# Attention scores and values issued for four units at a time, with ScalarE's work reordered around them, in a top-k attention and MLP kernel

## The chip, the cores and the metric

The kernel runs on one core of a Trainium2 chip. A core has a matmul engine (TensorE, PE in the profile, with its weight loads listed as PEld), a vector engine (VectorE, DVE), a scalar engine (ScalarE, ACT), a third elementwise engine (GpSimd, POOL) and a sync engine (SP) that issues transfers. They run side by side, each through its own instructions in order, and wait for each other on semaphores. The metric is the device time of one execution in microseconds (us): less is better.

## The reference

Two blocks follow one another. The attention has 8 batches, 8 heads, 576 tokens and 64 values per head, and keeps the 32 largest scores of every row. Its output, with the heads side by side, is the input of an MLP with 4608 tokens, 512 inputs, 2048 hidden values and a leaky ReLU. All is float32.

```python
def _attn_ref(q, k, v):                       # each (8, 8, 576, 64)
    scores = scale * np.matmul(q, k.transpose(0, 1, 3, 2))
    kth = np.partition(scores, -32, axis=-1)[..., -32:-31]
    scores = np.where(scores >= kth, scores, -1000000000.0)
    scores = scores - np.max(scores, axis=-1, keepdims=True)
    attn = np.exp(scores)
    attn = attn / (np.sum(attn, axis=-1, keepdims=True) + 1e-09)
    return np.matmul(attn, v).astype(np.float32)

def _moe_ref(x, w_in, w_out):                 # (4608, 512), (512, 2048), (2048, 512)
    h = x @ w_in
    g = np.maximum(0.01 * h, h)
    return (g @ w_out).astype(np.float32)
```

## The kernel before

The work is cut into 144 **units**. A unit is 128 rows of queries for two heads of one batch (a "pair" of heads), so two score blocks of 128 x 576. As 576 is four times 128 and 64 over, each batch also has two units of 64 rows for four heads. The MLP takes its tokens in 19 **chunks**, two of 128 and then 17 of 256; a chunk of 256 tokens needs the values of eight units.

One loop runs over steps. In step s, DVE picks the top 32 of unit s, POOL masks unit s-1, ACT takes its exponents, and unit s-2 is normalized, split in 16-bit halves, written out and read back transposed (wT). The values of a unit come some steps later. In between, the MLP is fed in small pieces: a budget says how much of it PE gets at each of the seven places ("slots") of a step. Each engine receives its instructions in the order in which the program names them.

Scores go to PSUM in two parts per unit, a "wide" (352 keys) and a "narrow" one (224 keys), and ACT copies them to SBUF. PSUM holds two "wide" buffers of two banks each, one "narrow" one of two banks, and two banks for the MLP. The values use one bank of a "wide" buffer too:

```python
    def scores(us):                                   # two units
        narrow = ps_sc.tile([P, 2, 512], F32, name="narrow")
        ps = {}
        for k, u in enumerate(us):
            wide = ps_sc.tile([P, 2, 512], F32, name="wide", bufs=2)
            ps[u] = ((wide[:, :, 0:WIDE], 0, WIDE),
                     (narrow[:, :, k * NARROW:(k + 1) * NARROW], WIDE, S))
        order = ((us[0], 0), (us[0], 1), (us[1], 1), (us[1], 0))
        for u, part in order:
            ...
                    nc.tensor.matmul(to[r0:r0 + u.rows, i, :], qt[d, u.q0:u.q0 + u.rows],     # L220
                                     kt[d, k0:k1], start=True, stop=True)
        for u in us:
            u.both = work.tile([P, 2, S], F32, name="s_sb", bufs=5)
            ...
        for u, part in order:
            nc.scalar.copy(u.both[:, :, k0:k1], to)                                          # L227

    def top_k(u):              # DVE; four parts, each ended by a yield
        ...                    # max and min of the halves of a row (L250), then four times
                               # MAX8 (L255), with MATCH_REPLACE8 (L258) between them
    def mask(u, i): ...        # POOL, L266 to L269
    def exponents(u, i): ...   # ACT, L272: exp(s_sb), and its sum z
    def sums(u): ...           # ACT, L277: ze = z + 1e-9
    def reciprocals(u): ...    # DVE, L281: rz = 1 / ze
    def normalize(u, i): ...   # ACT, L284: s_sb * rz

    def transpose(u):
        for h in range(2):
            split = work.tile([P, 2 * S], U16, name="split", bufs=2)
            nc.scalar.copy(split, pairs[:, :, h])                                            # L293
            nc.sync.dma_start(apart[:, h, :], split)
        u.wT = work.tile([P, 2 * NKC - 1, P], F32, name="wT", bufs=3)
        nc.sync.dma_start_transpose(out=u.wT.bitcast(U16), in_=...)                          # L296

    def weigh_values(u, po): ...   # PE, L333: 2 x 5 products of wT and v, two side by side
    def keep_values(u, po): ...    # ACT, L347: po to x, the MLP's input

    def mlp(ch):                   # a generator: one piece up to each yield
        for f0 in range(0, NFC, 2):
            ph = ps_ml.tile([P, 2, CHMAX], F32, name="ph", tag="ml")
            ...                    # PE, L389: 4 pieces of ph
            nc.scalar.activation(gT[...], ph[...], AF.Prelu, alpha=SLOPE)                    # L395
            yield 2 * max(n, 225)
        for r0 in range(0, n, P):
            pz = ps_ml.tile([P, 512], F32, name="pz", tag="ml")
            ...                    # PE, L401: 8 pieces of pz
            nc.scalar.copy(o_sb[0:m], pz[0:m, 0:DMODEL])                                     # L410
```

The schedule, from step 20 on (`HURRY` = 20; earlier steps differ in order, not in work):

```python
    def values_at(n):                        # step and place of unit n's values
        if n < UNHURRIED: return (n | 1) + LAG + 1, MIDDLE
        return (n | 1) + LAG - ((n | 1) in HURRIED), END             # LAG = 3

    def slot_budget(s):
        after = [at for (at, _), _ in ready_at if at >= s]           # when chunks become ready
        until = after[0] if after else s
        if len(after) >= len(CHUNKS) - EARLY: return EARLY_SHARE
        return backlog[0] / ((until + 1 - s) * SLOTS)                # SLOTS = 7

        for s in range(len(steps) + LAG + 1):
            cur, old, older, new = unit(s), unit(s - 1), unit(s - 2), ()
            if s % 2 == 0:
                new = [u for u in steps[s + 2:s + 4] if u]
            ...
            slot()                           # one part of top_k(cur)
            if old: mask(old, 0); mask(old, 1)
            if older: weights_of(older)      # reciprocals, normalize twice
            mlp_steps(budget)
            ...
            slot()
            mlp_steps(budget)
            if old: exponents(old, 0)
            if older: transpose(older)
            slot()
            mlp_steps(budget); mlp_steps(budget)
            slot()
            mlp_steps(budget)
            if old: exponents(old, 1); sums(old)
            keep(values(s, END), s, END)     # two units' values, and their copies to x
            if new: scores(new)              # two units' scores
            budget = slot_budget(s + 1)
            mlp_steps(budget); mlp_steps(budget)
            load_more(s)
```

Before the loop, the MLP's weights are rounded in 16 pieces (`round_weights`, on POOL, ACT, DVE and PE).

Of the kernel before, what the change touches and what calls it, by code (L numbers as in the profile page):

```python
# [20 lines left out]
def kernel(  # L21
# [37 lines left out]
    const = ctx.enter_context(tc.tile_pool(name="const", bufs=1))  # L59
    xpool = ctx.enter_context(tc.tile_pool(name="xpool", bufs=2))  # L60
    loads = ctx.enter_context(tc.tile_pool(name="loads", bufs=LOADED))
    raws = ctx.enter_context(tc.tile_pool(name="raws", bufs=3))
    work = ctx.enter_context(tc.tile_pool(name="work", bufs=2))
    small = ctx.enter_context(tc.tile_pool(name="small", bufs=5))
    halves = ctx.enter_context(tc.tile_pool(name="halves", bufs=3, space=bass.MemoryType.DRAM))
# [15 lines left out]
    w_out = [const.tile([P, 4, DMODEL], F32, name=f"w_out{c}") for c in range(NFC // 4)]  # L81
    gT = const.tile([P, NFC, CHMAX], F32, name="gT")

    NPIECE = 2 * HP * DFF // WCH
# [3 lines left out]
    def piece(n):  # L90
# [4 lines left out]
        f = 2 * (n - NPIECE // 2)  # L95
        return w_out[f // 4][:, f % 4:f % 4 + 2, :].rearrange("p g n -> p (g n)")

    raw_of = {}

    def load_weights(n):  # L100
        if n >= NPIECE:
            return
        if not AS_WORDS:
            nc.sync.dma_start(piece(n), weights[n])
            return
        raw_of[n] = raws.tile([P, WCH, 4], U16, name="raw")
        nc.sync.dma_start(raw_of[n].rearrange("p n w -> p (n w)"), weights[n])

    def round_weights(n):

        raw = raw_of.pop(n)
        dst = piece(n)
        mid = raw[:, :, 2]
        low = raw.rearrange("p n w -> p (n w)").bitcast(U32).rearrange("p (n w) -> p n w", w=2)[:, :, 0]
        top = raws.tile([P, WCH], U16, name="top", bufs=2)
        scale = raws.tile([P, WCH], U16, name="scale", bufs=2)  # L120
        parts = work.tile([P, 2 * NKC - 1, P], F32, name="wT", bufs=3)
        parts = parts.rearrange("p c n -> p (c n)").bitcast(U16)
        m_top, m_low = parts[:, 0:WCH], parts[:, WCH:2 * WCH].bitcast(BF16)
        nc.gpsimd.tensor_copy(top, raw[:, :, 3])
        nc.scalar.activation(dst, mid, AF.Copy, bias=-7.0 - 2.0 ** -16, scale=2.0 ** -20)

        nc.scalar.activation(m_low, low, AF.Copy, bias=128.0, scale=2.0 ** -29)
        yield
        nc.vector.tensor_scalar(scale, top, 4, 0x7FF, ALU.logical_shift_right, ALU.bitwise_and)  # L129
        if n < NPIECE - 2:  # L130

            nc.scalar.activation(scale.bitcast(BF16), scale, AF.Exp, bias=least, scale=LN2)
        else:

            nc.vector.tensor_scalar(scale, scale, 1151.0, 896.0, ALU.min, ALU.max)
            nc.vector.tensor_scalar(scale, scale, 896.0, 128.0, ALU.subtract, ALU.mult)
        nc.vector.tensor_scalar(m_top, top, 0xF, 0x3F80, ALU.bitwise_and, ALU.bitwise_or)
        nc.vector.tensor_scalar(top, top, 0x8000, None, ALU.bitwise_and)  # L138
        if n < NPIECE - 4 or n % 2 == 0:
            tag, bufs = ("wide", 2) if n < NPIECE - 4 else ("narrow", 1)  # L140
            pw = ps_sc.tile([P, 2, 512], F32, name=tag, bufs=bufs)
            sums = [(pw[:, h, :], h * 512) for h in range(2)]
            ends = [(pw.rearrange("p h n -> p (h n)"), 0)]
        else:
            ends = sums = [(ps_ml.tile([P, 512], F32, name="pw", tag="ml"), h * 512) for h in range(2)]
        for pw, c in sums:
            at = slice(c, c + 512)
            nc.tensor.matmul(pw, ident_top, m_top[:, at].bitcast(BF16), start=True, stop=False)
            nc.tensor.matmul(pw, ident, dst[:, at], start=False, stop=False)
            nc.tensor.matmul(pw, ident_low, m_low[:, at], start=False, stop=True)  # L150
        yield
        nc.vector.tensor_tensor(scale, scale, top, ALU.bitwise_or)  # L152
        for pw, c in ends:
            at = slice(c, c + pw.shape[-1])
            nc.vector.tensor_tensor(dst[:, at], pw, scale[:, at].bitcast(BF16), ALU.mult)  # L155
# [5 lines left out]
    def load_qk(pi):  # L161
        if pi % (LOADED + 3) < LOADED:
            qt = loads.tile([P, S], F32, name="qt")
            kt = loads.tile([P, S], F32, name="kt")
        else:
            raw = raws.tile([P, WCH, 4], U16, name="raw").rearrange("p n w -> p (n w)").bitcast(F32)
            qt, kt = raw[:, 0:S], raw[:, S:2 * S]
        nc.sync.dma_start(qt, qT[pi])
        nc.sync.dma_start(kt, kT[pi])
        qk_of[pi] = qt, kt  # L170
# [32 lines left out]
    def scores(us):  # L203
# [16 lines left out]
                    nc.tensor.matmul(to[r0:r0 + u.rows, i, :], qt[d, u.q0:u.q0 + u.rows],  # L220
                                     kt[d, k0:k1], start=True, stop=True)
        for u in us:
            u.both = work.tile([P, 2, S], F32, name="s_sb", bufs=5)
            u.s = [u.both[:, i, :] for i in range(2)]
        for u, part in order:
            to, k0, k1 = ps[u][part]
            nc.scalar.copy(u.both[:, :, k0:k1], to)  # L227
# [1 line left out]
    def first_scores(u):  # L229

        ps = [ps_sc.tile([P, 2, 512], F32, name="wide", bufs=2) for i in range(2)]
        for half in range(2):
            for i, pi, side, r0 in u.parts:
                qt, kt = qk_of[pi]
                d = slice(side * D, (side + 1) * D)
                nc.tensor.matmul(ps[i][:, half, 0:HS], qt[d, u.q0:u.q0 + P],
                                 kt[d, half * HS:(half + 1) * HS], start=True, stop=True)
        u.both = work.tile([P, 2, S], F32, name="s_sb", bufs=5)
        u.s = [u.both[:, i, :] for i in range(2)]
        for i in range(2):  # L240
            nc.scalar.copy(u.s[i].rearrange("p (h n) -> p h n", h=2), ps[i][:, :, 0:HS])

# [40 lines left out]
    def normalize(u, i):  # L283
        nc.scalar.activation(u.s[i], u.s[i], AF.Copy, bias=0.0, scale=u.rz[:, i:i + 1])  # L284

    def transpose(u):


        pairs = u.both.rearrange("p i n -> p (i n)").bitcast(U16).rearrange("p (n h) -> p n h", h=2)
# [1 line left out]
        for h in range(2):  # L291
            split = work.tile([P, 2 * S], U16, name="split", bufs=2)
            nc.scalar.copy(split, pairs[:, :, h])  # L293
            nc.sync.dma_start(apart[:, h, :], split)
        u.wT = work.tile([P, 2 * NKC - 1, P], F32, name="wT", bufs=3)
        nc.sync.dma_start_transpose(out=u.wT.bitcast(U16), in_=apart.rearrange("p h n -> (p h) n"))  # L296

    def transpose_in_haste(u):
# [8 lines left out]
            u.parts_T.append((c0, c1, pt))  # L307

    def keep_transposed(u):
        u.wT = work.tile([P, 2 * NKC - 1, P], F32, name="wT", bufs=3)  # L310
        for c0, c1, pt in u.parts_T:
            nc.scalar.copy(u.wT[:, c0:c1, :], pt[:, 0:c1 - c0, :])

# [37 lines left out]
    def hidden_of_few(ch, x):  # L351

        g_of = {}
        for j in range(NFC // 4):
            ph = ps_ml.tile([P, 512], F32, name="ph", tag="ml")
            for c in range(HP):
                nc.tensor.matmul(ph, x[c][:, 0:P], w_in[c][:, j * 512:(j + 1) * 512],
                                 start=(c == 0), stop=(c == HP - 1))
                if c == 1:
                    yield 2 * 512  # L360
            g_of[j] = raws.tile([P, 2 * DMODEL], U16, name="scale", bufs=2).bitcast(F32)
            nc.scalar.activation(g_of[j], ph, AF.Prelu, alpha=SLOPE)  # L362
            yield 2 * 512
            if j:
# [77 lines left out]
    HURRIED = (15, 23, 31)  # L442
    HASTY = (14, 15, 23, 31)
    UNHURRIED = 14
    MIDDLE, END = 0, 1

    def values_at(n):

        if n < UNHURRIED:
            return (n | 1) + LAG + 1, MIDDLE  # L450
        return (n | 1) + LAG - ((n | 1) in HURRIED), END
# [17 lines left out]
                ready.append(ch)  # L469
                backlog[0] += mlp_cost(ch)  # L470

    def slot_budget(s):

        after = [at for (at, _), _ in ready_at if at >= s]
        until = after[0] if after else s
        if len(after) >= len(CHUNKS) - EARLY:
            return EARLY_SHARE
        return backlog[0] / ((until + 1 - s) * SLOTS)

    EARLY_SHARE = 500  # L480
    SLOTS = 7

    with tc.manual_schedule():
        last = {p: n for n, u in enumerate(steps) for p in u.pairs}

        def load_more(s):

            for of, load, n, lag in ((v_of, load_v, LOADED_V, LAG + 1), (qk_of, load_qk, LOADED + 3, 8)):
                while len(of) < NPAIR and (len(of) < n or last[len(of) - n] + lag <= s):
                    load(len(of))  # L490
                    if lag > LAG + 1 and len(of) > n:
                        break


        for n in range(3):
            load_weights(n)
        rounding = {}
        for n in range(NPIECE + 2):
            for i in (n, n - 1, n - 2) if AS_WORDS else ():
                if 0 <= i < NPIECE:  # L500
                    if i == n:
                        rounding[i] = round_weights(i)
                    next(rounding[i], None)
            load_weights(n + 3)
# [15 lines left out]
        def values(*place):  # L520
            due = [u for n, u in enumerate(steps) if values_at(n) == place]
            if due:
                po = ps_sc.tile([P, 2, 512], F32, name="wide", bufs=2)[:, 0, 0:2 * P]
                po = po.rearrange("p (u n) -> p u n", u=2)
            else:
                return ()
            for n, u in enumerate(due):
# [7 lines left out]

        for s in range(len(steps) + LAG + 1):
            cur, old, older, new = unit(s), unit(s - 1), unit(s - 2), ()
            if s % 2 == 0:
                new = [u for u in steps[s + 2:s + 4] if u]
            picks = top_k(cur) if cur else iter(())  # L540
            budget = slot_budget(s)

# [7 lines left out]
            if old:  # L550
                mask(old, 0)
                mask(old, 1)
            late = s < HURRY and not {s - 1, s - 2} & set(HURRIED)
            if older and not late and not at_first:
                weights_of(older)
            mlp_steps(budget)
# [7 lines left out]
            if s - 2 in HASTY:  # L564
                transpose_in_haste(older)
            mlp_steps(budget)
            if old:
                exponents(old, 0)
            if older:
                keep_transposed(older) if s - 2 in HASTY else transpose(older)  # L570
            slot()
            mlp_steps(budget)
            mlp_steps(budget)
            slot()
            mlp_steps(budget)
            if old:
                exponents(old, 1)
                sums(old)
            if not at_once:
                keep(weighed, s, MIDDLE)  # L580
            if new and s < HURRY:
# [2 lines left out]
            if new and s >= HURRY:  # L584
                scores(new)
            budget = slot_budget(s + 1)
            mlp_steps(budget)
            mlp_steps(budget)
            load_more(s)
        mlp_steps(1e9)  # L590
# [58 lines left out]
```

## Time and profile before

| | |
|---|---|
| time, median of three runs | 1474.29 us (1473.32 to 1475.12) |
| span of the profiled run | 1471.0 us |
| mean granted clock of PE | 0.979 |
| bytes moved | 222.29 MB, mean 151 GB/s |
| median from issue to landing: split out, transposed back | 2.1 us, 4.6 us |

The profile lists one execution. A line such as L333 is a line of the kernel; a group is written as line, engine, operation, output<-input, shapes, count. PE lists every float32 matmul twice[...]. The table by stage gives, for each stretch of time, the busy time of PE, PEld, DVE, ACT and POOL with the number of instructions, then the granted clock, the share of the transfer engines and GB/s. The timeline gives start, length, engine, line and count, and in brackets how long the engine had been idle before and who released it. A line of the waits names who waited, for whom, how long in all, how often and the longest. The ends of matmuls are modelled, so PE is better read from start to start.

### The profile page before, as it was taken

The numbers are of one execution on the slowest core, as the hardware profiler recorded it, in microseconds if no ns is written. First come the engines' busy times: TensorE is split into PE (matmuls) and PEld (weight loads), VectorE is DVE, ScalarE is ACT, GpSimd is POOL, SyncE is SP. The second block draws the span as 40 slices with busy tenths as digits, with TensorE's granted clock in tenths as the row PEclk, the third lists the DMA queues.
The fourth block names the chain that finished last, engine by engine and source line by source line (L and its number), as shares of the span: only waits on it lengthen the run. The fifth ranks groups of instructions, "written<-read, shape, count | busy, mean of one in ns | idle before, by whom it ended". The sixth has DMA issues, their size and how long they took to land.

```text
span 1471.0 us, 24094 instructions
## 1 busy us (share of the span) xinstructions
PE 1395.6 (95%) x8066; PEld 928.7 (63%) x8068; DVE 1322.4 (90%) x3400; ACT 1095.7 (74%) x1979; POOL 1096.5 (75%) x743
## 2 busy tenths in 40 slices
PE   7717989999999999999999999999999999999999
PEld 2304547676766666666666666767676767676674
DVE  7999999999999999999999999999999999999600
ACT  8657877877787777777777777787877787877720
POOL 3188877888788888787878788878787888787700
PEclk9957999999999999999999999999999999999999
DMA  9725443654367554666557545565457555654510
GB/s 343 287 73 137 137 113 89 172 168 137 105 169 214 131 147 130 182 175 152 137 164 198 154 128 144 161 198 144 130 164 207 143 134 130 170 136 134 145 47 14
DMA packets 388795, 222.29 MB, mean 151 GB/s; under 512 B 333888, under 2 KB 333888, under 8 KB 386624
## 3 DMA queue, kind: packets, MB, share of 16 engines
q1 hardware_dynamic: 388672, 220.77, 53.1%
q8 instruction: 63, 1.03, 0.3%
q14 instruction: 60, 0.49, 0.1%
HBM read 46.14 MB, written 92.01 MB: 94 GB/s over the span
## 4 chain that ended last, share of the span: by engine, by line
PE 86%; DVE 11%; DMA 1%; ACT 1%; issue 1%; POOL 0%; DVEq 0%; SPq 0%; ACTq 0%
PE pz L401 33%; PE ph L389 32%; PE wide L333 11%; PE wide L220 6%; DVE tops L255 4%; PE narrow L220 3%; DVE pairs L258 3%; DMA raw<-in_weights_dram 1%; DVE pairs L250 1%; DVE w_in L155 1%; DVE scale L152 1%; DMA wT<-apart 0%; DVE w_out L155 0%; DVE scale L129 0%; DVE top L138 0%
## 5 line engine op out<-in xcount | busy, mean ns | idle before, releaser
L268 POOL TENSOR_SCALAR pen<-s_sb,tops 128x576 f32<-128x576 f32 x288 | 637.5, 2213 | 209.6 <-DVE tops L255 116.8
L255 DVE MAX8 tops<-pairs 128x8 f32<-128x288 f32 (+1 forms) x1152 | 636.5, 592 | 0.0
L401 PE MATMUL pz<-w_out,gT 128*128 128x512 f32 x1152 | 510.7, 597 | 4.9 <-ACT scale L362 4.9
L389 PE MATMUL ph<-x,w_in 128*128 128x256 f32 x2176 | 481.1, 381 | 0.0
L258 DVE MATCH_REPLACE8 pairs<-tops,pairs 128x288 f32<-128x288 f32 (+1 forms) x864 | 460.6, 539 | 0.0
L389 PEld LDWEIGHTS ph<-x,w_in 128*128 128x128 f32 x2176 | 410.7, 190 | 77.1 <-issue 22.9
L269 POOL TENSOR_TENSOR s_sb<-s_sb,pen 128x576 f32<-128x576 f32 x288 | 406.9, 1413 | 24.1
L401 PEld LDWEIGHTS pz<-w_out,gT 128*128 128x128 f32 x1152 | 215.6, 190 | 269.7 <-issue 263.5
L293 ACT COPY split<-s_sb 128x1152 uint16<-128x1152 uint16 x280 | 306.9, 1145 | 0.0
L284 ACT ACTIVATE s_sb<-s_sb,rz 128x576 f32<-128x576 f32 x288 | 207.0, 769 | 42.2 <-DVE rz L281 42.2
L272 ACT ACTIVATE s_sb<-s_sb,nbias 128x576 f32<-128x576 f32 x288 | 221.0, 767 | 12.5 <-POOL s_sb L269 12.5
L250 DVE TENSOR_TENSOR pairs<-s_sb 128x576 f32<-128x576 f32 x288 | 213.4, 780 | 9.9
L333 PEld LDWEIGHTS wide<-wT,vt 128*64 128x64 f32 x3200 | 161.7, 139 | 65.5 <-ACT s_sb L227 27.0
L333 PE MATMUL wide<-wT,vt 128*64 128x128 f32 (+1 forms) x3200 | 179.0, 268 | 22.8 <-ACT s_sb L227 21.2
L395 ACT ACTIVATE gT<-ph 128x512 f32<-128x512 f32 x136 | 80.6, 592 | 80.1 <-PE ph L389 80.1
L347 ACT COPY x<-wide 128x128 f32<-128x128 f32 (+1 forms) x160 | 32.1, 260 | 128.2 <-PE wide L333 128.2
L227 ACT COPY s_sb<-wide 128x704 f32<-128x704 f32 x142 | 107.2, 755 | 25.4 <-PE wide L220 25.3
L220 PE MATMUL wide<-kt,qt 64*128 64x352 f32 (+1 forms) x392 | 76.5, 504 | 26.5 <-ACT s_sb L227 23.6
L227 ACT COPY s_sb<-narrow 128x448 f32<-128x448 f32 x142 | 68.7, 537 | 1.3 <-PE narrow L220 0.6
L410 ACT COPY o_sb<-pz 128x512 f32<-128x512 f32 x36 | 21.1, 585 | 59.2 <-PE pz L401 59.2
L281 DVE RECIPROCAL rz<-ze 128x2 f32<-128x2 f32 x144 | 22.5, 156 | 46.1 <-ACT ze L277 45.9
L258 DVE MATCH_VALUE_LOAD pairs<-tops,pairs 128x8 f32 x864 | 63.4, 73 | 0.0
(63 smaller groups left out, 620.5 us busy)
## 6 DMA issues: line engine op xcount, KB each, us to landing
apart<-split SPq DMA_DIRECT2D x280, 288.0 KB, 2.1
raw<-in_weights_dram SPq DMA_DIRECT2D x16, 1024.0 KB, 7.2
vt<-in_vk_dram SPq DMA_DIRECT2D x32, 320.0 KB, 3.5
out_dram<-o_sb SPq DMA_DIRECT2D x36, 256.0 KB, 2.0
qt<-in_qT_dram SPq DMA_DIRECT2D x20, 288.0 KB, 3.1
kt<-in_kT_dram SPq DMA_DIRECT2D x20, 288.0 KB, 3.5
raw<-in_qT_dram SPq DMA_DIRECT2D x12, 288.0 KB, 3.1
raw<-in_kT_dram SPq DMA_DIRECT2D x12, 288.0 KB, 3.6
```

Source lines behind the costliest of these rows:

```text
L220: nc.tensor.matmul(to[r0:r0 + u.rows, i, :], qt[d, u.q0:u.q0 + u.rows], kt[d, k0:k1], start=True, stop=True)
L250: nc.vector.tensor_tensor(pairs[:, :, n, :], u.both[:, :, 0:HS], u.both[:, :, HS:S], op)
L255: nc.vector.max(out=u.tops[:, i, r, :], in_=rest[i])
L258: nc.vector.match_replace(out=rest[i], in_to_replace=u.tops[:, i, r, :], in_values=rest[i], imm_value=LOWEST)
L268: nc.gpsimd.tensor_scalar(pen, u.s[i], u.tops[:, i, ROUNDS - 1, 7:8], MASKED, ALU.is_lt, ALU.mult)
L269: nc.gpsimd.tensor_tensor(u.s[i], u.s[i], pen, ALU.add)
L272: nc.scalar.activation(u.s[i], u.s[i], AF.Exp, bias=u.nbias[:, i:i + 1], scale=SCALE, accum_out=u.z[:, i:i + 1])
L284: nc.scalar.activation(u.s[i], u.s[i], AF.Copy, bias=0.0, scale=u.rz[:, i:i + 1])
L293: nc.scalar.copy(split, pairs[:, :, h])
L333: nc.tensor.matmul(po[side * D:(side + 1) * D, o, :], vt[:, c, side, :], u.wT[:, c + side * NKC if c + 1 < NKC else c, r:r + n], start=(c ...
L389: nc.tensor.matmul(ph[:, i, 0:n], w_in[c][:, f * P:(f + 1) * P], x[c][:, 0:n], start=(c == 0), stop=(c == HP - 1),)
L401: nc.tensor.matmul(pz[0:m, 0:DMODEL], gT[:, f, r0:r0 + m], w_out[f // 4][:, f % 4, :], start=(f == 0), stop=(f == NFC - 1),)
```

## The change

Scores and values of the units from 40 on come in groups of four. In every fourth step, after the second slot, a block is issued: the scores of the next two units, the values of four finished units (those still go to one "wide" buffer, whose bank they now fill), then the scores of two more. Into this block, in ACT's order, are put the splits of unit s-2 and the exponents of unit s-1, so that ACT has work while PE makes the values, and the copies of the values right behind. The purpose is to change less often between the shapes of matmul, and to keep ACT from standing idle at the values. The budget counts in slots rather than steps, and the pieces of the MLP stand between ACT's single operations.

To have room for more units in flight, the buffers that the weights' rounding leaves free (`words`, `tops_scales`) serve later as two more wT buffers, a sixth score buffer and the extra buffers for q and k, which were rotating tiles before. Cut to its core:

```diff
+    words = raws.tile([P, 3, WCH * 4], U16, name="words")
+    tops_scales = raws.tile([P, 4, WCH], U16, name="tops_scales")
+    later = ...                                    # five buffers within words
+    wT_bufs = [three tiles] + [two of later]       # unit n uses wT_bufs[n % 5]
+    s_bufs = [five tiles] + [one in tops_scales]   # n % 6 from unit 30 on, n % 5 before
 ...
-        nc.gpsimd.tensor_copy(top, raw[:, :, 3])       # round_weights: ahead of ACT's two
+        nc.gpsimd.tensor_copy(top, raw[:, :, 3])       # behind them, in a part of its own
 ...
-    def transpose(u):
+    def transpose(u, between):
             nc.scalar.copy(split, pairs[:, :, h])
             nc.sync.dma_start(apart[:, h, :], split)
+            if h == 0:
+                between()
 ...
+    MIDDLE, END, AMID = 0, 1, 2
+    FOURS = 40
     def values_at(n):
+        if n >= FOURS - 4:
+            return ((n | 1) if len(steps[n].pairs) > 1 and n % 4 < 2 else (n | 3)) + LAG + 1, AMID
 ...
-    def slot_budget(s):
+    def slot_budget(s, done=0):
+        ends = [at * SLOTS + (SLOTS_AHEAD if place == AMID else SLOTS) for (at, place), _ in ready_at]
+        left = [end - s * SLOTS - done for end in ends if end > s * SLOTS + done]
 ...
+        return backlog[0] / (left[0] if left else SLOTS)
+    SLOTS_AHEAD = 2
 ...
-            if s % 2 == 0:
-                new = [u for u in steps[s + 2:s + 4] if u]
+            if s % 2 == 0 and s + 2 < FOURS:
+                new = steps[s + 2:s + 4]
+            four = s % 4 == 3 and s + 1 >= FOURS
 ...
-            late = s < HURRY and not {s - 1, s - 2} & set(HURRIED)
+            late = s < HURRY and not {s - 1, s - 2} & set(HURRIED) or s % 4 == 0 and s >= FOURS
             if older and not late and not at_first:
                 weights_of(older)                  # with late: behind the second slot
             mlp_steps(budget)
 ...
             mlp_steps(budget)
-            if old: exponents(old, 0)
-            if older: ... transpose(older)
+            if four:
+                if unit(s + 1):
+                    scores(steps[s + 1:s + 3])
+                weighed = values(s, AMID)
+                if older:
+                    transpose(older, lambda: None)
+                if old:
+                    exponents(old, 0)
+                keep(weighed, s, AMID)
+                if old:
+                    exponents(old, 1)
+                    sums(old)
+                if unit(s + 3):
+                    scores(steps[s + 3:s + 5])
+                budget = slot_budget(s, SLOTS_AHEAD)
+                mlp_steps(budget)
+                mlp_steps(budget)
+            else:
+                if old:
+                    exponents(old, 0)
+                mlp_steps(budget)
+                keep(values(s, AMID), s, AMID)
+                if older: ... transpose(older, lambda: mlp_steps(budget))
+            slot()
             slot()
             mlp_steps(budget)
-            mlp_steps(budget)
-            slot()
-            mlp_steps(budget)
-            if old:
+            if old and not four:
                 exponents(old, 1)
                 sums(old)
+            mlp_steps(budget)
```

## The prediction

> **What bounds the kernel now.** I read the page first, then the busy time by stage, then the timeline of the matmul engine over one turn, then the waits.
>
> ```profile
> PE 1395.6 (95%) x8066; PEld 928.7 (63%) x8068; DVE 1322.4 (90%) x3400; ACT 1095.7 (74%) x1979; POOL 1096.5 (75%) x743
> PE 86%; DVE 11%; DMA 1%; ACT 1%; issue 1%; POOL 0%; DVEq 0%; SPq 0%; ACTq 0%
> ```
>
> PE is busiest and 86% of the chain that ended last. The table by stage (PE, PEld, DVE, ACT, POOL busy) shows where:
>
> ```profile
> 80.00:120.00 40.00, 10.84 (x70) 8.19 (x72) 39.62 (x101) 26.75 (x49) 33.26 (x24) 0.54 0.38 104
> 754.20:901.70 147.50, 147.50 (x866) 100.54 (x865) 141.50 (x369) 116.28 (x212) 119.71 (x81) 1.00 0.58 159
> ```
>
> Until about 200 us DVE (top-k) is full and PE has little to do; after that PE never idles, and DVE is free for only 6.0 of 147.5 us (16 units), about 0.37 us per unit. The change acts almost wholly in this second stage. One turn there, and the last MLP piece in the chain:
>
> ```profile
> 827.84 11.39 PE L389 MATMUL ph<-x,w_in 128*128 128x256 f32 x52
> 839.16 2.40 PE L333 MATMUL wide<-wT,vt 128*64 128x128 f32 x40
> 841.49 0.86 PE L220 MATMUL wide<-kt,qt 64*128 64x352 f32 x4
> 842.19 0.92 PE L220 MATMUL narrow<-kt,qt 64*128 64x224 f32 x8
> 842.94 0.76 PE L220 MATMUL wide<-kt,qt 64*128 64x352 f32 x4
> 843.63 14.94 PE L389 MATMUL ph<-x,w_in 128*128 128x256 f32 x68
> ...
> 1412.41 27.63 PE ph L389 x128
> 1440.04 27.48 PE pz L401 x64
> ```
>
> Read from start to start. 256 columns take 27.63/128 = 0.216 us and 512 take 27.48/64 = 0.429 us, so a column takes 0.834 ns plus 2.4 ns per matmul. A pair of values (20 times two side by side, 128 columns) should then take 20 x 0.109 = 2.18 us; it takes 841.49 - 839.16 = 2.33. A pair of scores (four matmuls of 352 and four of 224 columns, each beside its twin) should take 1.94; it takes 2.14. The MLP run of 52 takes 11.32 for 11.23, that of 68 (to the next values at 858.50) 14.87 for 14.68: about 0.1 us at each end. So a turn loses 0.15 + 0.20 + 0.19 = 0.54 us in its three changes of shape, 0.18 each. Check: a chunk of 256 tokens (8 units) should take 27.63 + 27.48 + 4 x (2.18 + 1.94) + 4 x 0.54 = 73.8 us, and 16 units take 147.5.
>
> Now who waits for whom inside that stage (ACT's and DVE's timelines, then the waits from 606.65 to 1197.2):
>
> ```profile
> 833.21 0.77 ACT L272 ACTIVATE s_sb<-s_sb,nbias 128x576 f32<-128x576 f32 x1
> 833.87 0.19 ACT L272 ACTIVATION_READ_ACCUMULATOR s_sb<-s_sb,nbias 128x1 f32 x1
> 834.10 0.20 ACT L277 ACTIVATE ze<-z 128x2 f32<-128x2 f32 x1
> ...
> 834.33 0.17 DVE L281 RECIPROCAL rz<-ze 128x2 f32<-128x2 f32 x1 [1.06 <-ACT ze L277]
> ...
> ACT x L347 <- PE wide L333: 65.0, 32, 3.1
> DVE rz L281 <- ACT ze L277: 19.9, 30, 1.2
> ```
>
> DVE's spare time is spent waiting for ze, the sum that ACT makes at the end of a step: DVE is tied to ACT, and ACT (in program order) to PE.
>
> **What the Trainium skill says.** "TensorEngine Tiling (Array Packing)", section Key Properties: changing the tiling mode drains the engine. The trace agrees: 0.18 us per change, as above. "TensorE: Matmul & The Clock Gate", in its section on the array of 32x32 parts: ScalarE and VectorE queues are strict FIFO, matmuls stay in program order. The trace agrees: at 834.33 the reciprocal waits 1.06 us and the MAX8 behind it, which needs no ze, waits too. "PSUM — Partial Sum Buffer", Specifications: a bank holds 512 FP32 values per partition; so the values of four units (4 x 128 columns) fill the one bank used of a "wide" buffer. No run shows that yet.
>
> **The change, part by part.**
>
> *Fewer changes of shape.* For units 40 to 143 a block is scores of two, values of four, scores of two: four changes of shape for four units, where two turns have six. Units 36 to 143 (values) and 40 to 143 (scores) now take 52 turns x 3 and two of values alone x 2 = 160 changes. After: the block at step 39 has scores alone (2), the 25 at 43 to 139 have 4, the values of a half-group at 57, 93 and 129 stand alone (2 each), the last two blocks 3: 111. So 49 x 0.18 = **8.8 us** less work for PE. A block takes 2 x 2.14 + 40 x 0.109 + 0.15 = 8.8 us, and four units take 27.6 (half a chunk of MLP) + 8.8 + 0.2 = 36.5 us.
>
> *Uneven steps.* The MLP is dealt out in 7 slots a step, 55.1/56 = 0.98 us of PE each. Now every second step has 6.9 us of PE, the others 11.5. After, three steps of 6.9 us follow one of 15.7, while DVE still needs 8.9 us for each. Take T as the start of the block in step s (s = 43, 51, ...: the MLP half that makes ph follows), and follow the chain:
> - PE starts MLP at T + 8.9 and ends the third ph tile (3.46 us each) at T + 19.3.
> - Counting pieces by the new budget, that tile's Prelu is emitted in slot 5 of step s+1, just ahead of the second exponent and ze. ACT: wait 0.2, Prelu 0.49, exponent with sum 0.89, ze 0.2: ze at T + 21.0. Even without this Prelu, the one before it (T + 16), an exponent 0.76, two splits 2.10, exponent and ze give T + 20.4.
> - DVE's reciprocal in step s+2 waits for it. From there DVE has no pause: rest of that step 5.9, step s+3 8.9, first slot of step s+4 3.0: its reciprocal is at T + 38.9.
> - ACT needs that one for the two normalizations (1.34) which stand ahead of the block of step s+4, then the last Prelu (0.49), then the copy of the first scores (0.75): T + 41.7.
> - Only then is a "wide" buffer free for the values. PE would start them at T + 36.5 + 2.1 = T + 38.7. **PE waits 3.0 us.** If the Prelu falls one slot later, 2.4; if the last Prelu is already done, 0.5 less. I take 2.4, from 1.8 to 3.1.
>
> In the half that makes pz there is no Prelu: ACT runs through the block, two norms, exponent, splits and exponent and has ze near T + 17 to 19, when DVE is at T + 20: no wait. So one stall per chunk, at steps 47, 55, ..., 135: 12. At 143 no scores stand before the values. 12 x 2.4 = **+29 us**, from 22 to 37.
>
> In the kernel before the same reckoning leaves room: the reciprocal ahead of a turn lies one DVE step after a ze made before the previous turn, and ACT does wait for PE at x (65.0 us in 32 times), down to 0.40 us in the ph half.
>
> *The rest.* Named buffers in place of rotating ones: no work. Weights: POOL's copy is emitted later, but it waited for the same DVE instruction before; +-1 us. Five wT buffers for three let transposes start earlier; PE did not wait for them. Before step 36 budgets stay as they were. At the end, x copies directly ahead of the last chunk: +0.7 us.
>
> Sum: 1474.3 - 8.8 + 29 + 0.7 = **1495 us**.
>
> **Rivals.**
> - *The saving alone*: ACT and DVE keep pace, PE never waits: 1474.3 - 8.8 + 0.7 = 1466 us. For it: PE has not waited for data since 200 us in the kernel before, and the new order puts splits and exponents exactly into the 4.5 us of the values. Against: the chain above, in which only DVE's 17.8 us for two steps has to be right.
> - *A stall at every block*: 23 x 3 us, 1535. For it: the steps are as uneven in the pz half. Against: no Prelu there ties ACT to PE, and DVE's lag has shrunk by the previous stall.
> - *The values wait for wT*: four wT must lie ready at once, after two writes of 2.1 us and a transposing read of 4.6 us. For it: one such wait is in the chain now (5.22 us at 397.14). Against: the last of the four is split two steps, 15 us, before its block. One or two us per block would make 1490 to 1520.
>
> **Range and chances.** I give the chain through DVE six chances in ten (1487 to 1509), the saving alone three and a half (1462 to 1475). The point lies in the first; the range takes both, 1464 to 1509. Over 2% slower begins at 1503.8: 0.22. Faster by over 2% would need 1445, more than all the changes of shape could give: 0.01.
>
> **What would show it.** Right: value runs of four, about 4.5 us; waits of PE or PEld at wide L333 for ACT's s_sb copy, about 12 of 2 to 3 us, near steps 47, 55, ...; reciprocals waiting 4 to 5 us for ze once per chunk; a chunk takes 75.5 us, and 73.1 without the stall. Wrong: PE fully busy with 73.1 us per chunk (first rival), stalls twice a chunk, or stalls put down to DMA wT. A ze in the ph half before T + 18 would break my chain at its second link.

## The result and the profile after

The changed kernel takes 1521.76 us (median; 1520.59 to 1525.41) against 1474.7 us: a ratio of 1.0324, 95% interval 1.0305 to 1.0344. It is slower, and lies 12.8 us above the upper end of the range foreseen.

Three words are used below. A **block** is named by its step: the one of step 43 is the first with values of four units, and further ones follow every four steps. The **ph half** and the **pz half** are the two halves of a chunk's MLP, so every second block stands where a ph half ends and a pz half begins. The blocks of steps 59, 95 and 131 are **half-filled**: the values in them are those of two units of 64 rows only.

The page of the profile after, engines and shares of the chain:

```profile
PE 1403.6 (92%) x8066; PEld 942.1 (62%) x8068; DVE 1323.7 (87%) x3400; ACT 1086.6 (71%) x1979; POOL 1095.8 (72%) x743
PE 49%; DVE 33%; ACT 12%; issue 4%; DMA 1%; POOL 0%; DVEq 0%; ACTq 0%; POOLq 0%
```

The number of instructions is as before, and DVE's and ACT's busy times are within 1% of it; what changed is the chain. PE held 86% of it and now holds 49%, DVE 33% for 11%: long stretches of the end time are now set by DVE and ACT. By stage, two whole chunks (16 units) of the settled part:

```profile
703.31:859.59 156.28, 149.78 (x834) 104.91 (x832) 141.94 (x369) 115.00 (x213) 119.68 (x81) 0.98 0.54 152
```

They take 156.3 us for 147.5 before. PE is idle for 6.5 of them (none before) and its granted clock is 0.98 (1.00 before). The block of step 71, between a ph half and a pz half, PE's timeline:

```profile
731.14 0.86 PE L243 MATMUL wide<-kt,qt 64*128 64x352 f32 x4
731.83 0.92 PE L243 MATMUL narrow<-kt,qt 64*128 64x224 f32 x8
732.59 0.76 PE L243 MATMUL wide<-kt,qt 64*128 64x352 f32 x4
736.13 1.76 PE L356 MATMUL wide<-words,vt 128*64 128x128 f32 x20 [2.79 <-ACT s_sb L249]
737.67 4.71 PE L356 MATMUL wide<-wT,vt 128*64 128x128 f32 x60
742.32 0.86 PE L243 MATMUL wide<-kt,qt 64*128 64x352 f32 x4
```

The scores end at 731.14 + 2.14 = 733.28 and the values start at 736.13: PE waits 2.85 us for ACT's copy of the scores (L249). Then the values take 742.32 - 736.13 = 6.19 us, where four units take 4.52 in the blocks at full clock. What ACT and DVE did meanwhile, in order of time (normalizations are L305, reciprocals L302):

```profile
713.98 0.60 ACT L418 ACTIVATE gT<-ph 128x512 f32<-128x512 f32 x1
714.47 0.77 ACT L293 ACTIVATE s_sb<-s_sb,nbias 128x576 f32<-128x576 f32 x1
715.36 0.20 ACT L298 ACTIVATE ze<-z 128x2 f32<-128x2 f32 x1
...
715.59 0.17 DVE L302 RECIPROCAL rz<-ze 128x2 f32<-128x2 f32 x1 [3.92 <-ACT ze L298]
724.48 0.15 DVE L302 RECIPROCAL rz<-ze 128x2 f32<-128x2 f32 x1
733.34 0.15 DVE L302 RECIPROCAL rz<-ze 128x2 f32<-128x2 f32 x1
...
733.52 1.44 ACT L305 ACTIVATE s_sb<-s_sb,rz 128x576 f32<-128x576 f32 x2 [2.60 <-DVE rz L302]
734.87 0.57 ACT L418 ACTIVATE gT<-ph 128x512 f32<-128x512 f32 x1
735.35 0.73 ACT L249 COPY s_sb<-wide 128x704 f32<-128x704 f32 x1
```

This is the chain foreseen, link by link. Its T is 694.12, the start of the previous block (step 67): ze ends at T + 21.4 (foreseen 21.0), the third reciprocal is at T + 39.2 (38.9), the score copy ends at T + 42.0 (41.7). DVE waits 3.92 us for ze, and two steps later ACT waits 2.60 us for DVE, with the score copies that PE needs standing behind it.

The three waits of this chain over the whole execution, in the kernel before:

```profile
DVE rz L281 <- ACT ze L277: 45.9, 52, 6.9
ACT s_sb L284 <- DVE rz L281: 42.2, 48, 5.4
PEld wide L333 <- ACT s_sb L227: 27.0, 7, 14.6
```

and now:

```profile
ACT s_sb L305 <- DVE rz L302: 122.0, 75, 5.5
DVE rz L302 <- ACT ze L298: 93.4, 40, 7.2
PEld wide L356 <- ACT s_sb L249: 83.6, 32, 14.6
```

The profiled execution of the changed kernel took 1525.41 us, 3.7 more than the median, so the account that follows explains a little more than the 47.1 us between the medians. Reading all blocks from start to start, the 52.6 us between the two profiled spans (1523.6 and 1471.0) come out as:

| what | us |
|---|---|
| 12 waits before the values, ph half to pz half (1.55 to 2.86 each) | +30.1 |
| waits in the first two blocks, steps 39 (scores alone) and 43: 1.5 and 7.2 | +8.7 |
| values of 6 blocks partly at half the clock (1.7 to 3.0 each) | +11.8 |
| small waits in the other blocks (0.39 to 1.12 before the values, 1.0 at the second scores of three half-filled blocks) | +9.4 |
| the end: the last values, and x before the last chunk | +0.8 |
| changes of shape saved, as worked out ahead | -8.8 |
| sum | +52.0 |

### The profile page after: what moved, and what is told of

Same layout as the page of the kernel before. It is cut to its first block, busy times and chain, and to the rows that moved or that the text cites. A ratio compares the mean times of both kernels' runs of the same rounds, so it can differ in the third digit from the quotient of the medians.

```text
span 1523.6 us, 24085 instructions
## 1 busy us (share of the span) xinstructions
PE 1403.6 (92%) x8066; PEld 942.1 (62%) x8068; DVE 1323.7 (87%) x3400; ACT 1086.6 (71%) x1979; POOL 1095.8 (72%) x743
## 4 chain that ended last, share of the span: by engine, by line
PE 49%; DVE 33%; ACT 12%; issue 4%; DMA 1%; POOL 0%; DVEq 0%; ACTq 0%; POOLq 0%
PE pz L424 20%; DVE tops L276 15%; PE ph L412 14%; DVE pairs L279 12%; PE wide L356 10%; ACT split L314 4%; DVE pairs L271 4%; PE wide L243 3%; ACT s_sb L293 2%; ACT s_sb L249 2%; PE narrow L243 2%; ACT s_sb L305 1%; DMA words<-in_weights_dram 1%; ACT gT L418 1%; DVE w_in L178 1%
## 5 line engine op out<-in xcount | busy, mean ns | idle before, releaser
L289 POOL TENSOR_SCALAR pen<-s_sb,tops 128x576 f32<-128x576 f32 x250 | 553.3, 2213 | 217.1 <-DVE tops L276 121.3
L290 POOL TENSOR_TENSOR s_sb<-s_sb,pen 128x576 f32<-128x576 f32 x250 | 352.7, 1411 | 20.9
L305 ACT ACTIVATE s_sb<-s_sb,rz 128x576 f32<-128x576 f32 x250 | 180.5, 772 | 122.0 <-DVE rz L302 122.0
L314 ACT COPY split<-s_sb 128x1152 uint16<-128x1152 uint16 x242 | 267.0, 1153 | 0.0
L271 DVE TENSOR_TENSOR pairs<-s_sb 128x576 f32<-128x576 f32 x250 | 186.6, 785 | 7.8 <-DVE tops L276 0.5
L356 PE MATMUL wide<-wT,vt 128*64 128x128 f32 (+1 forms) x1920 | 115.8, 280 | 51.2 <-ACT s_sb L249 51.2
L356 PEld LDWEIGHTS wide<-wT,vt 128*64 128x64 f32 x1920 | 106.1, 147 | 69.5 <-ACT s_sb L249 63.9
L289 POOL TENSOR_SCALAR pen<-tops_scales,tops 128x576 f32<-128x576 f32 x38 | 84.1, 2213 | 40.0 <-ACT split L314 28.3
L302 DVE RECIPROCAL rz<-ze 128x2 f32<-128x2 f32 x144 | 22.3, 155 | 93.5 <-ACT ze L298 93.4
L249 ACT COPY s_sb<-wide 128x704 f32<-128x704 f32 x123 | 92.1, 749 | 4.6 <-PE wide L243 4.6
L356 PE MATMUL wide<-words,vt 128*64 128x128 f32 (+1 forms) x1280 | 75.5, 274 | 14.0 <-ACT s_sb L249 12.9
L356 PEld LDWEIGHTS wide<-words,vt 128*64 128x64 f32 x1280 | 69.0, 145 | 24.6 <-ACT s_sb L249 19.6
```

The costliest lines, as they stand in the source:

```text
L271: nc.vector.tensor_tensor(pairs[:, :, n, :], u.both[:, :, 0:HS], u.both[:, :, HS:S], op)
L289: nc.gpsimd.tensor_scalar(pen, u.s[i], u.tops[:, i, ROUNDS - 1, 7:8], MASKED, ALU.is_lt, ALU.mult)
L290: nc.gpsimd.tensor_tensor(u.s[i], u.s[i], pen, ALU.add)
L356: nc.tensor.matmul(po[side * D:(side + 1) * D, o, :], vt[:, c, side, :], u.wT[:, c + side * NKC if c + 1 < NKC else c, r:r + n], start=(c ...
```

## The experiments

Theory A is the chain above: PE waits because score copies stand in ACT's queue behind normalizations that wait for a late reciprocal. Theory B: ACT has too much work in the block, in whatever order. Theory C: the cost is not in the groups of four at all but in the named buffers and the spread pieces. The medians are given with the ratio to the kernel before on the same chip and its 95% interval.

**Normalizations behind the first score copies.** In the block steps the reciprocal keeps its place and the two normalizations move:

```diff
+            if older and four:
+                reciprocals(older)
-            if older and not late and not at_first:
+            elif older and not late and not at_first:
                 weights_of(older)
 ...
             if four:
                 if unit(s + 1):
                     scores(steps[s + 1:s + 3])
+                if older:
+                    normalize(older, 0)
+                    normalize(older, 1)
                 weighed = values(s, AMID)
```

> In the block steps alone, ACT's two normalizations stand behind the first pair of scores copies instead of ahead of the block; DVE's reciprocal stays where it was. Theory A (PE waits because ACT's score copies queue behind normalizations that wait for a late reciprocal): the twelve waits of 2.3 to 2.9 us between first scores and values go, and with them the stretches of half clock; in exchange the x copies come some 0.4 us late per block. 1476 us (1468 to 1486), with some 4 us of wait left at step 43. Theory B (ACT simply has too much work in the block): the same work in another order still makes PE wait, at the second scores instead, 2 us or more in each block of the ph half; 1505 to 1525 us. Theory C (the cost lies in the other parts, named buffers and spread pieces): no change, 1515 to 1525.

Measured: 1482.58 us, ratio 1.0051 (1.0035 to 1.0067). 39 us of the 47 are gone with the same work on every engine. The same block as above from its last scores on, PE's timeline and then ACT's:

```profile
717.21 0.76 PE L243 MATMUL wide<-kt,qt 64*128 64x352 f32 x4
717.90 1.31 PE L356 MATMUL wide<-words,vt 128*64 128x128 f32 x20
719.04 3.44 PE L356 MATMUL wide<-wT,vt 128*64 128x128 f32 x60
722.41 0.86 PE L243 MATMUL wide<-kt,qt 64*128 64x352 f32 x4
```

```profile
718.27 0.77 ACT L249 COPY s_sb<-wide 128x704 f32<-128x704 f32 x1
718.91 1.46 ACT L305 ACTIVATE s_sb<-s_sb,rz 128x576 f32<-128x576 f32 x2
```

The values follow the scores at once and take 722.41 - 717.90 = 4.51 us, at full clock. The waits, over the whole execution:

```profile
ACT s_sb L305 <- DVE rz L302: 97.2, 71, 5.5
PEld wide L356 <- ACT s_sb L249: 43.9, 32, 14.6
```

ACT still waits 97.2 us for late reciprocals, but the score copies no longer stand behind them, and PE's weight loads wait 39.7 us less for those copies. So here the wait for a reciprocal costs little by itself; what costs is what stands behind it. A holds and B, in its strong form, falls. What is left of B: 0.32 us at the second scores of most blocks, 2.1 us at the three half-filled ones; and the block of step 43 still waits 3.8 us, and its values take 7.19 us.

**Pairs only.** All of the change except the groups:

```diff
-    FOURS = 40
+    FOURS = 200
```

> The changed kernel with the groups of four turned off for all units: named buffers, spread pieces, new budget and reordered weight rounding stay. Theory A and B: as the kernel before, 1474 us (1468 to 1482). Theory C: most of the 47 us stay, over 1495.

Measured: 1471.86 us, ratio 0.9987 (0.998 to 0.9993). C falls: the named buffers and the spread pieces cost nothing, and bring 2 us (1.0 to 2.9).

**One top-k round less**, in the changed kernel and in the kernel before. It keeps the 24 largest scores of a row in place of 32, so part of the computation is left out:

```diff
-    TOPK = 32
+    TOPK = 24
-            rest = [pairs[:, i, 0, :] if r < ROUNDS // 2 else
+            rest = [pairs[:, i, 0, :] if r < 2 else
```

> The changed kernel with one round of the top-k left out (24 largest instead of 32, and the third round over whole rows is the last one): DVE needs some 6.3 us a step in place of 8.9. It leaves out part of the computation. Theory A: two DVE steps are 5 us shorter, so the reciprocal is in time and the waits between first scores and values vanish; then the groups of four gain what they save, and this is 5 to 12 us faster than the kernel before with the same round left out. Theory B: ACT's work is the same, so the waits stay: 20 us or more slower than that kernel.

> The kernel before with the same round of the top-k left out, as the measure for the other one. PE bounds it from about 200 us on either way, so only the first stage, which DVE bounds, gets shorter: some 12 steps of 2.6 us, and less where PE then has no work yet; 1440 to 1460 us.

Measured: 1454.57 us (ratio 0.9865, 0.985 to 0.988) and 1465.24 us (ratio 0.9937, 0.9921 to 0.9952), both against the kernel before with all its rounds. PE's timeline at the same block of the changed kernel with this DVE:

```profile
695.86 0.86 PE L243 MATMUL wide<-kt,qt 64*128 64x352 f32 x4
696.56 0.92 PE L243 MATMUL narrow<-kt,qt 64*128 64x224 f32 x8
697.31 0.76 PE L243 MATMUL wide<-kt,qt 64*128 64x352 f32 x4
698.00 1.31 PE L356 MATMUL wide<-words,vt 128*64 128x128 f32 x20
```

No wait, with ACT's order and work as in the change. So the late link is DVE's time. The block of step 43 loses nothing here either: its scores start at 438.74 and its values at 440.88.

With DVE out of the way the changed kernel is 10.7 us faster than the one before. Less the 2 us that the rest of the change brings, that is 8.7 us, where the count of shape changes gave 8.8; so close a match is partly luck. The traces show 4.0 of the 10.7 us ahead of the first group already (one turn of values starts at 406.03 in place of 410.06), and in the half-filled blocks PE still waits 2.9 us in all for the copies to x. The cleaner measure is a chunk of the settled stage: from block to block it takes 768.95 - 695.86 = 73.09 us here, and 73.75 in the kernel before, which is 8.6 us over 13 chunks.

The kernel before gained only 9 us, too little for the range expected. Its table by stage shows why, in the first stage (DVE's busy time third, POOL's fifth):

```profile
120.00:160.00 40.00, 34.38 (x175) 19.62 (x176) 29.60 (x83) 33.55 (x63) 37.88 (x25) 0.89 0.47 134
```

DVE is busy for 29.6 of 40 us only, and POOL, with its mask, for 37.9. POOL seems to take DVE's place as the bound there; no run takes work off POOL to show it.

**The second exponent ahead of the fifth slot's MLP pieces**, and so ahead of the Prelu at the head of the chain:

```diff
             slot()
             slot()
-            mlp_steps(budget)
             if old and not four:
                 exponents(old, 1)
                 sums(old)
             mlp_steps(budget)
+            mlp_steps(budget)
```

> The changed kernel, but the second exponent and the sum stand ahead of the fifth slot's MLP pieces and so ahead of the third ph tile's Prelu. If the late chain begins at that Prelu, ze comes 0.6 us earlier (the exponents and splits before it then set it) and the waits of 2.9 us become 2.3, as in the chunks where the Prelu already falls a slot later; fewer of them fall to half clock: 1510 us (1503 to 1517). If the chain began elsewhere (DVE alone, or transfers), no change: 1519 to 1525.

Measured: 1514.72 us, ratio 1.0268 (1.0254 to 1.0282). The six waits of 2.86 us became 2.27, all of them, as a chain that begins at that Prelu would have it. That is 3.5 of the 7 us gained; the rest was not traced. By the prediction's reckoning the remaining 2.3 us come from the exponents and splits that ACT does before; no run takes these away. The slow turns of values did not become fewer, as I had expected: 6 of the 11 waits of 2.27 us are followed by one, and in the changed kernel it was 5 at the same 11 blocks.

**The first values early.** Units 36 to 39 keep the steps of the kernel before:

```diff
-        if n >= FOURS - 4:
+        if n >= FOURS:
```

> The changed kernel, but the values of units 36 to 39 come at steps 40 and 42 as in the kernel before, instead of together in the block of step 43; the normalizations stay ahead of the block. If the 7.2 us that PE waits in the block of step 43 come from too little MLP work between steps 39 and 43 (one chunk stretched over ten steps, the next one ready a step later), they shrink to the 2 to 3 us of the other blocks: 1512 us (1507 to 1517). If they come from the block's order alone, nothing changes: 1520 to 1524.

Measured: 1518.7 us, ratio 1.0292 (1.0276 to 1.0308), 3 us less than the change and 7 more than expected, between the two forecasts. My reason for the loss at the first blocks does not hold. PE's timeline there:

```profile
448.65 1.31 PE L356 MATMUL wide<-words,vt 128*64 128x128 f32 x20
452.85 2.37 PE L356 MATMUL wide<-words,vt 128*64 128x128 f32 x20 [2.89 <-DMA words<-apart]
455.15 2.55 PE L424 MATMUL pz<-w_out,gT 128*128 128x512 f32 x4
```

The wait came back at another place, for the transposed weights of unit 39: the units themselves are late. The kernel with pairs only has two long turns of values at the same time (2.90 us at 434.60 and 3.58 at 451.86, for 2.33), with waits for transposed weights. And DVE, which makes the units, has no time to spare there. The table by stage of the kernel before shows it (DVE's busy time third):

```profile
400.00:440.00 40.00, 39.42 (x255) 26.77 (x253) 39.69 (x102) 33.51 (x62) 33.35 (x23) 1.00 0.65 174
480.00:520.00 40.00, 40.00 (x210) 25.48 (x209) 39.62 (x101) 32.28 (x59) 33.26 (x24) 1.00 0.52 133
```

DVE is as full between 400 and 520 us as it was before 200 us; only later does it have 6 of 147.5 us free. The groups begin at about 423 us, in the middle of that stretch.

**Groups of four later.** To see whether that lag is the cause, the change with the groups starting at unit 112:

```diff
-    FOURS = 40
+    FOURS = 112
```

> The changed kernel with groups of four from unit 112 on in place of 40. Three blocks of the ph half then still wait before their values (2.5 us each, and 3 us for half clock), small waits 2 us, and some 15 changes of shape are saved (2.7 us), on top of 1472 us for pairs only. If the 12 us lost at the first blocks come from DVE being behind PE just then (at 440 us the kernel with pairs makes PE wait for wT too), they shrink here, where DVE has caught up: 1484 us (1479 to 1488). If they are the price of going over to groups of four as such, they stay: 1493 us (1489 to 1498).

Measured: 1486.96 us, ratio 1.0087 (1.0072 to 1.0103). Within the range of the lag, outside that of a fixed price. The first full block's wait, the 7.2 us one in the change, is 3.1 here, and its values take the usual 4.52 us:

```profile
1122.55 2.40 PE L356 MATMUL wide<-words,vt 128*64 128x128 f32 x40 [3.09 <-ACT s_sb L249]
```

A part of the price stays, though: in the change the block of this step (115), long after the start, waits only 0.4 us. Why is open.

**Repairs.** With the normalizations moved as above, ACT now copies the values to x ahead of the exponents too, and ahead of the splits where the block has only two units of values:

```diff
+                if len(weighed) < 4:
+                    keep(weighed, s, AMID)
                 if older:
                     transpose(older, lambda: None)
-                if old:
-                    exponents(old, 0)
-                keep(weighed, s, AMID)
+                if len(weighed) == 4:
+                    keep(weighed, s, AMID)
                 weighed = ()
                 if old:
+                    exponents(old, 0)
                     exponents(old, 1)
```

> As the run with the normalizations behind the first score copies, and besides ACT copies the values to x ahead of both exponents, and in blocks with only two units of values ahead of the splits too. Theory A with ACT's order inside the block as the rest: the 0.32 us that PE waits at the second scores of 22 blocks go, and the 2.2 us at the three blocks with half the values shrink below 0.5: 12 us less than that run, 1471 us (1466 to 1476). If ACT's total work in the block were the limit, no change against it: 1480 to 1484.

Measured: 1468.42 us, ratio 0.996 (0.9946 to 0.9974): 0.4% faster than the kernel before, little, but clear of the noise. Its blocks lose nothing from step 47 on; that of step 43 still waits 3.8 us, and its values take 7.24. The same with the first values early:

> All three together: normalizations behind the first score copies, x copies ahead of the exponents, first values early. What is left is the saving in changes of shape against the kernel with pairs only: 10 us below 1472, so 1463 us (1458 to 1468), faster than both kernels.

Measured: 1469.9 us, ratio 0.9959 (0.9946 to 0.9971), not to be told from the one without, and above the range expected. As above, that edit moves the first loss rather than ending it. And the repaired kernel with the groups from unit 64 on, when DVE is no longer full:

> The kernel with normalizations behind the first score copies and x copies ahead of the exponents, with groups of four from unit 64 on. It gives up a quarter of the saving (2.5 of 10 us). If DVE's lag at 440 us causes the loss at the first blocks, most of that loss goes (5 to 8 us): 1464 us (1460 to 1467). If going over costs the same anywhere: 1471 us (1469 to 1475).

Measured: 1464.66 us, ratio 0.9935 (0.9923 to 0.9948), the fastest of those that do the whole work. Its first full block from the last scores on, PE's timeline:

```profile
673.21 0.76 PE L243 MATMUL wide<-words 64*128 64x352 f32 x4
673.90 3.50 PE L356 MATMUL wide<-wT,vt 128*64 128x128 f32 x60
```

No wait. With the run with one round less, this shows that the loss at the first blocks depends on DVE's state at that time: it goes when DVE has less to do, and when the groups begin later in the repaired kernel.

## Why the prediction was wrong, point by point

The direction and the main mechanism were right; the sum was 27 us short.

- *Fewer changes of shape, 8.8 us.* About right: 0.66 us less per chunk, 8.6 us in all. (The trace has 112 changes for the 111 counted, as the last two turns of values have two each.)
- *Uneven steps and the chain.* Right in each link, to within half a microsecond. Two edits took the waits away (normalizations moved, DVE shortened), and one made them shorter (exponent moved).
- *12 stalls of 2.4 us, 29 us.* 12 waits with 30.1 us, at the steps foreseen.
- *"One stall per chunk."* This is the step that failed. It took the wait as the whole price and the end of the ph half as the only place. Three terms were missing, 29.9 us together. The values also ran partly at half the clock in 6 of the 12 blocks with a wait over 2 us (11.8 us). PE waited 8.7 us in the first two blocks: T was reckoned from a settled state that the kernel had not reached at step 43. The small waits of the next point make 9.4 us. The second term could have been seen in the profile before: I read DVE as full until about 200 us and with time to spare after, and PE as never waiting, but DVE is full again from 400 to 520 us, and in the kernel before PE already waits for wT at 402 us.
- *"In the half that makes pz there is no Prelu ... no wait."* Nearly right: DVE had caught up a little less than I reckoned. At the block at 694.12 the normalization ended 1.3 us into the block, and PE waited 0.39 us; with the larger waits of the half-filled blocks this is 9.4 us. I had treated those blocks like the others, though their values last only 2.5 us. At the second scores PE then waits for the copy to x, which stands in ACT's order behind the splits and an exponent; with that copy moved ahead the wait is gone.
- *The rest.* The named buffers and the spread pieces bring 2 us; I had put them at nothing.
- *The rivals.* The saving alone, to which I gave three and a half chances in ten, is near what the repaired order comes to: 1464.66 us against 1466. That is partly luck, as the repaired kernel has fewer groups and the 2 us of the rest. A stall of 3 us at every block did not come. In the changed kernel PE waits for no wT at the blocks; it does so when the first values are made earlier.

## What to carry to other kernels

Where engines work through their queues in order and one step's work is spread over several of them, a reordering that makes the steps of one engine uneven must be followed through all the others: add up, from each link that waits, how long the slower engine needs to the next meeting point, and compare it with the time that the faster one now leaves. Whatever must wait for a late engine belongs in the queue behind what another engine is about to need. And a wait on PE can cost more than its length: here about half of those over 2 us were followed by values at a lower clock, which cost as much as 3.0 us more.

## What the hardware did that I had not expected

Waits of 2.2 to 3.2 us on PE, each after 25 us or more of full work, were often followed by half the granted clock. The stages within the values at 736.13 of the changed kernel (granted clock third from the end):

```profile
736.10:737.70 1.60, 1.57 (x22) 1.57 (x24) 1.60 (x5) 1.60 (x4) 1.46 (x2) 0.73 0.00 0
737.70:739.90 2.20, 2.20 (x24) 2.20 (x23) 2.10 (x4) 2.20 (x3) 1.21 (x1) 0.50 0.19 71
740.40:742.30 1.90, 1.90 (x38) 1.74 (x32) 1.90 (x8) 0.06 (x1) 1.82 (x2) 1.00 0.44 164
```

Half the clock for some 3.4 us, then full again, though PE did not pause in between. It does not follow every such wait. In the four runs that keep the normalizations ahead of the block and all rounds (the change, the exponent moved, the first values early, the groups late), slow values follow 10 of 15 waits of 2.8 to 3.2 us and 11 of 21 waits of 2.2 to 2.3 us. After the four longer waits, 3.8 and 7.2 us at step 43, they came each time; of the turns of values that directly followed their scores without a wait, 116 over all runs with groups, none was slow. So the waits go with the half clock, and within this range their length hardly tells; what decides it is not settled by these runs.
